# A tuned FFT and two-layer-pair kernel: conversion blocks in other slots, a conversion's buffers in alternating roles, a copy of the first quad and some GpSimd tasks at other places

## The chip, the cores and the metric

The kernel runs on one core of one Trainium2 chip. The metric is the device time of one execution in microseconds (us). The engines are PE (TensorE), DVE (VectorE), ACT (ScalarE), POOL (GpSimd) and SP (SyncE, which here only issues DMAs).

## What is computed

The reference, cut to what matters:

```python
X = np.fft.fft(np.fft.fft(x, axis=1), axis=2).real        # x: 4 x 3072 x 256
xk = mu_k * X + (1 - mu_k) * X_prev                       # X_prev: X one token earlier
xr = mu_r * X + (1 - mu_r) * X_prev
k = np.maximum(xk @ w_k, 0)                               # 256 -> 1024
y = sigmoid(xr @ w_r) * (k * k @ w_v)                     # 1024 -> 256
h = y @ w_in                                              # 256 -> 2048
out = (h - np.tanh(h)) @ w_out                            # 2048 -> 256
```

The weight matrices w_k, w_r, w_v, w_in and w_out reach the chip as 64-bit floats and are turned into 32-bit floats there.

## The kernel before, in words

**Stages.** A first stage does the transform (up to about 98 us). Phase 1 (98 to 678 us) does the layer with w_k, w_v and w_r, phase 2 (678 us to the end) the layer with w_in and w_out. Both phases work on 12 pairs of token blocks (2 x 512 tokens). A pair is done in quads, 4 in phase 1 and 8 in phase 2; a quad is a 2 x 2 block product with seven sub-products instead of eight, whose left operands are called a11, a12, a22, s1, s2, s3, s4, and then the four products of the second matrix ("11", "12", "21", "22"), which for a quad are issued during the next one. Every sub-product is three matmuls (`mm3`, L318 to L320): each operand is split into a rounded part, "hi", made by an ACT cast, and the rest, "lo", a subtraction on DVE or POOL.

**A quad's chain.** PSUM banks X, Z and W hold the sums. In the order of the program: a11 goes into X, ACT copies it (s1 copy, L504); a12 goes into Z, s2 into X, and ACT copies X again (s2 copy, L523); DVE adds the first copy to Z (L519); ACT applies the nonlinearity to Z (L482), DVE multiplies (L531), ACT rounds (hi, L487) and DVE subtracts (lo, L489). s3 goes into X, ACT copies it a third time (s3 copy, L539), and DVE adds it to W (L549), which gives the next block. a22 then goes into X and s4 into W. A bank is written anew only when its last reader is done. In the very first quad there is no previous quad's product to fill the gaps.

**Slots.** All work that is not the chain (operands of the next pair, weight conversions, loads) is put into slots: `at(slot, ...)` files a task, `fill()` runs the tasks of the next slot, four times per quad: after the s2 copy, after the lo of block 11, after the nonlinearity of block 22, and after the hi of block 22. So a phase 1 pair n has the slots n.0 to n.15, written here as pair.slot. Within a slot the conversions stand ahead of the tasks of the next pair. Each engine executes its own instructions strictly in the order in which they were written.

**Conversions.** `convert` with `fine=True` takes a block through seven steps: a load of four 128 KB pieces into the tile raw (SP, L364); the absolute value of the high words into tile a (ACT, L372); four DVE steps on a and raw (L374, L376, L378, L380; the last writes tile b); the scaled low words into b, the last reader of raw (DVE, L382); then in the next slot a + b (POOL, L392), and in the slot after that the write of a to DRAM (SP, L411; called keep). w_in has eight such blocks, w_out eight, and one block of w_v is done in pair 0. For w_in and that w_v block `x_room` gives one buffer of raw and one each of a and b (cva, cvb). The lists `early` and `free` (slots 0, 2, 6, 9 to 15 of each pair) say where the steps go.

**Pair 11** also prepares phase 2: `weights2` loads a w_in block into the tile wf (one buffer, SP L801) and a w_out block into another, and splits them (ACT L351, POOL L352 and L428 to L431, for the first two w_out blocks DVE L352); `left2` loads the stored pair (L791) and splits it (ACT L582, POOL L584; sums L592 to L595 on POOL).

**Pair 0's tasks.** `both_tasks` prepares the operands of pair n + 1: differences d0 to d3 (POOL L684), mixes k0 to k3 (DVE L689), scaled differences m0 to m3 (ACT L694), +0 to +3 (POOL L695), +s1 to +s4 (POOL L592 to L595), and the splits a11 to s4 (ACT L582, POOL L584) and x0 to x3 (ACT L351, POOL L352).

Of the kernel before, what the change touches and what calls it, by code (L numbers as in the profile page):

```python
# [7 lines left out]
F32 = mybir.dt.float32  # L8
# [314 lines left out]
def block(n, t):  # L323

    g, i = divmod(n, 6)
    m, j = divmod(i, 3)
    return (2 * g + t, 3 * m + 2) if j == 2 else (2 * g + j, 3 * m + t)


class Kernel:  # L330
    def __init__(self, tc, **dram):
        self.tc, self.nc = tc, tc.nc
        self.V, self.A, self.G, self.T = self.nc.vector, self.nc.scalar, self.nc.gpsimd, self.nc.tensor
        self.__dict__.update(dram)
        self.slots, self.now = {}, 0
        self.pend, self.odd = None, 0

    def at(self, slot, *stages):

        for k, f in enumerate(stages):  # L340
            if f:
                self.slots.setdefault(slot + k, []).append(f)
# [55 lines left out]
    def x_room(self):  # L398
        raw = self.xp.tile([128, 512, 2], I32, tag="raw", name="raw", bufs=1)
        def more():  # L400
            a, b = (self.xp.tile([128, 512], F32, tag=f"cv{x}", name=f"cv{x}", bufs=1) for x in "ab")
            return [a, b, b]
        return raw, more

# [62 lines left out]
    def quad(self, ph, n, q, nq, S, W, w2, done, extra=None):  # L467

        V, A, T = self.V, self.A, self.T
        ALU, ACT = mybir.AluOpType, mybir.ActivationFunctionType
        M = {}
        def P(ps, k, start, stop=True):
            i = RIGHT[k]
            mm3(T, ps, [W[:, 0, i], W[:, 1, i]], [S[k][:, 0], S[k][:, 1]], start, stop)
        bank = lambda tag, name: self.ps.tile([128, TOK], F32, tag=tag, name=name, bufs=1)
        ctile = lambda: self.act.tile([128, TOK], F32, tag="c", name="c", bufs=4)
        stile = lambda: self.act.tile([128, TOK], F32, tag="s", name="s", bufs=3)
        def bend(src):  # L480
            t = ctile()
            A.activation(t, src, ACT.Tanh if ph == 2 else ACT.Relu)  # L482
            return t
        gate = V.tensor_sub if ph == 2 else V.tensor_mul
        def hi(blk, g):
            M[blk] = self.act.tile([128, 2, TOK], F32R, tag="m", name=f"m{blk}", bufs=4)
            A.copy(M[blk][:, 0], g)  # L487
        def lo(blk, g):
            V.tensor_sub(M[blk][:, 1], g, M[blk][:, 0].bitcast(F32))  # L489
        p, self.pend = self.pend, None  # L490
        def late(*names):
            for k in names:
                if p:
                    p["late"][k]()
        self.odd ^= 1
        X, Z = bank(f"x{self.odd}", "x"), bank("z", "z")
        r = None
        P(X, "a11", True)
        if ph == 1:
            late("t21", "g21")  # L500
        else:
            late("t21", "c12", "g21")
        s1 = stile()
        A.copy(s1, X)  # L504
        if ph == 1:
            late("c12", "h21")
        else:
            late("t12", "h21", "g12")
        self.second(p, "11")
        P(Z, "a12", True)  # L510
        Wb = None
        if p is None:
            Wb = bank("w", "w")
            P(Wb, "s1", True)
        late("l21")
        if ph == 2:
            late("h12")
        P(X, "s2", False)
        V.tensor_add(Z, Z, s1)  # L519
        if ph == 2:  # L520
            late("l12")
        s2 = stile()
        A.copy(s2, X)  # L523
        if ph == 1:
            self.fill()
            late("t12", "g12")
        t11 = bend(Z)
        if ph == 2:
            self.fill()
        self.second(p, "22")  # L530
        gate(Z, Z, t11)  # L531
        if ph == 1:
            late("h12", "l12")
        P(X, "s3", False)
        hi("11", Z)
        if extra:
            r = extra(bank(f"x{1 - self.odd}", "r"))
        s3 = stile()
        A.copy(s3, X)  # L539
        lo("11", Z)  # L540
        self.fill()
        if r:
            r()
        if ph == 1:
            self.second(p, "21")
        if Wb is None:
            Wb = bank("w", "w")
            P(Wb, "s1", True)
        V.tensor_add(Z, Wb, s3)  # L549
        t22 = bend(Z)  # L550
        self.fill()
        self.second(p, "12")
        gate(Z, Z, t22)  # L553
        hi("22", Z)
        if ph == 1:
            self.fill()
            lo("22", Z)
        else:
            self.second(p, "21")
            lo("22", Z)  # L560
            self.fill()
        P(X, "a22", False)
        P(Wb, "s4", False)
        st = {}
        def t21():
            st["t21"] = bend(X)
        def c12():
            st["c12"] = Wb if ph == 1 else ctile()
            V.tensor_add(st["c12"], Wb, s2)
        def t12():  # L570
            st["t12"] = bend(st["c12"])
        self.pend = dict(n=n, q=q, nq=nq, m=M, w=w2, done=done, late=dict(
            t21=t21, c12=c12, t12=t12,
            g21=lambda: gate(X, X, st["t21"]), h21=lambda: hi("21", X), l21=lambda: lo("21", X),  # L574
            g12=lambda: gate(st["c12"], st["c12"], st["t12"]), h12=lambda: hi("12", st["c12"]), l12=lambda: lo("12", st["c12"])))  # L575
# [123 lines left out]
    def phase1(self):  # L699
        V, A, T = self.V, self.A, self.T  # L700
# [16 lines left out]
        def wv_task(q):  # L717
# [2 lines left out]
                t.append(self.kp.tile([128, TOK], F32, tag="xk", name="wv", bufs=4))  # L720
                self.nc.sync.dma_start(out=t[0], in_=self.wf[q])
            return [f, lambda: self.split(self.WV[q], t[0], self.G)]
        for r in (self.r0, self.r1):
            self.at(0, r[2])
        for q in range(3):
            self.at((0, 2, 6)[q], *wv_task(q))
        at = self.at
        for q, where in ((3, (0, 3, 5, 6, 8, 9, 10, 11)),):
            steps, out = self.convert(self.chunk_rows(self.wv, (q, q + 4)), [lambda a, q=q: self.split(self.WV[q], a, self.G)], self.x_room, V, True)
            for w, f in zip(where, steps + [lambda out=out: [f() for f in out]]):  # L730
                at(w, f)
        free = iter([16 * n + k for n in range(6, NP) for k in (0, 2, 6, 9, 10, 11, 12, 13, 14, 15)])
        for q in range(8):
            steps, out = self.convert(self.chunk_rows(self.w_out, (q, q + 8)), self.keep(12 + q), self.y_room, self.G, True)
            when = [next(free) for _ in steps[1:]]
# [4 lines left out]
        early = [16 * n + k for n in range(1, 6) for k in (0, 2, 6, 9, 10, 11, 12, 13, 14, 15)][2:]  # L740
        for q in range(8):
            steps, out = self.convert(self.quad_rows(self.w_in, q, HID2 // 2), self.keep(4 + q), self.x_room, self.G, True)
            when = early[8 * q:8 * q + 6] if q < 6 else [next(free) for _ in steps[1:]]
            at(early[8 * q - 3] + 1 if 0 < q < 6 else when[0] - 4, steps[0])
            for w, f in zip(when, steps[1:]):
                at(w, f)
            at(when[-1] + 1, *out)
        for n in range(NP):
            z = 16 * n
            if n == 0:  # L750
                for t, (f0, f1, f2) in ((3, self.r_task(0, 1, 0)), (4, self.r_task(0, 1, 1))):
                    at(t, f0, f1, f2)
            if n % 6 == 2:
                at(z + 4, lambda n=n: self.swap_rows(block(n, 1)[0]))
            if n + 1 < NP:
                u = self.both_tasks(n + 1)
                early = {0: "d0", 2: "d1", 4: "k0 d3", 5: "k1 m0", 6: "a11 d2 +0", 7: "k3 a12", 8: "k2 m1 a22", 9: "+s1 +1 m3"}
                if n == 0:
                    early = {0: "d0", 2: "d1", 4: "k0", 5: "k1 m0", 6: "a11 d3 +0", 7: "d2 a12", 8: "k3 m1", 9: "k2 a22 +1 m3 +s1"}
                for k, names in {**early, 10: "m2 s1 +s3 +3", 11: "+s2 +2", 12: "s3 +s4", 13: "s2", 14: "s4", 15: "x0", 16: "x1", 18: "x2", 19: "x3"}.items():  # L760
                    for name in names.split():
                        at(z + k, u[name])
                if n % 6 == 1:
                    at(z + 12, lambda n=n: self.swap_rows(block(n + 1, 0)[0]))
            for q in range(4):
                if n + 1 == NP and q == 1:
                    self.open2()
                w2 = [[self.WV[q][:, s, 256 * c:256 * c + 256] for s in range(2)] for c in range(2)]
                k = 4 * n + q - 1
                self.quad(1, n, q, 4, self.S[n], self.TK[q], w2, done, (lambda ps: r_block(ps, k)) if k >= 0 else None)  # L770
# [164 lines left out]
```

## Time and profile before

| | |
|---|---|
| median of 3 runs | 1674.95 us (1673.28 to 1676.17) |
| the profiled execution, whole | 1671.78 us |
| its span, first to last instruction | 1670.0 us |
| PE busy | 1633.8 us, 98% |
| DVE busy | 1274.7 us, 76% |
| ACT busy | 1135.8 us, 68% |
| POOL busy | 579.7 us, 35% |
| mean granted clock of PE | 0.992 of full speed |

The profile shows one execution, so its rows add up to its own time and not to the median. A row of the timeline has the start, the length, the engine, the line, the operation with output and input, and in brackets the idle time of the engine ahead of it and what ended that.

### The profile page before, as it was taken

How to read it: one execution, taken by the hardware profiler on the slowest of the kernel's cores; microseconds unless marked ns; L12 is line 12 of the kernel's file. 1: busy time of each engine (PE TensorE's matmuls, PEld its weight loads, DVE VectorE, ACT ScalarE, POOL GpSimd, SP SyncE). 2: the span in 40 equal slices, each digit the busy share in tenths (PEclk: the TensorE clock that was granted, in tenths of full speed). 3: DMA queues.
4: the chain of work that ended last, by engine and by line, in shares of the span. 5: the costliest groups of instructions: out<-in, count | busy, mean ns of one | idle time of the engine just before them, and what ended most of it. 6: DMA issues, size and time to landing. Idle time of an engine off the chain costs nothing.

```text
span 1670.0 us, 21330 instructions
## 1 busy us (share of the span) xinstructions
PE 1633.8 (98%) x7466; PEld 1352.9 (81%) x7466; DVE 1274.7 (76%) x2005; ACT 1135.8 (68%) x2162; POOL 579.7 (35%) x489
## 2 busy tenths in 40 slices
PE   7989999999999997999999999999999999999998
PEld 7967888888887885788888888888888888888887
DVE  7987888888888885777777777777777777777776
ACT  4876777777777775786666666666666666666665
POOL 0237676666667664481202020212112121212100
PEclk8999999999999998999999999999999999999999
DMA  9611001111111113211010101010101010101000
GB/s 328 160 41 39 32 33 45 45 58 45 64 46 63 35 35 108 82 39 51 1 51 1 51 1 51 1 51 1 51 1 51 1 51 1 51 1 51 1 26 26
DMA packets 39452, 77.96 MB, mean 47 GB/s; under 512 B 4512, under 2 KB 11808, under 8 KB 39344
## 3 DMA queue, kind: packets, MB, share of 16 engines
q1 hardware_dynamic: 37760, 72.41, 13.0%
q0 software_dynamic: 864, 3.41, 1.1%
q8 instruction: 58, 0.95, 0.2%
q10 hardware_dynamic: 720, 0.79, 0.1%
q14 instruction: 50, 0.41, 0.1%
HBM read 46.39 MB, written 30.20 MB: 46 GB/s over the span
## 4 chain that ended last, share of the span: by engine, by line
PE 92%; DVE 2%; issue 1%; ACT 1%; POOL 1%; DMA 1%; SPq 1%; ACTq 0%; DVEq 0%; POOLq 0%
PE o L319 15%; PE o L318 15%; PE o L320 15%; PE x L318 8%; PE x L319 8%; PE x L320 8%; PE w L318 4%; PE w L319 4%; PE w L320 4%; PE z L318 2%; PE z L319 2%; PE z L320 2%; PE r L319 1%; PE r L320 1%; PE r L318 1%
## 5 line engine op out<-in xcount | busy, mean ns | idle before, releaser
L489 DVE TENSOR_TENSOR m<-z,m 128x512 fp32r<-128x512 f32 x288 | 198.5, 689 | 139.6 <-ACT m L487 139.6
L319 PE MATMUL o<-m,WO 128*128 128x512 f32 x768 | 298.9, 389 | 0.0
L320 PE MATMUL o<-m,WO 128*128 128x512 f32 x768 | 298.8, 389 | 0.0
L318 PE MATMUL o<-m,WO 128*128 128x512 f32 x768 | 298.8, 389 | 0.0
L584 POOL TENSOR_TENSOR a<-xk,a 128x512 fp32r<-128x512 f32 x69 | 91.1, 1321 | 594.5 <-ACT a L582 592.7
L482 ACT ACTIVATE c<-z 128x512 f32<-128x512 f32 x288 | 172.9, 600 | 146.2 <-DVE z L549 145.6
L487 ACT CAST m<-z 128x512 fp32r<-128x512 f32 x288 | 169.2, 588 | 143.3 <-DVE z L553 79.7
L584 POOL TENSOR_TENSOR s<-xk,s 128x512 fp32r<-128x512 f32 x92 | 122.7, 1336 | 174.0 <-ACT s L582 174.0
L319 PEld LDWEIGHTS o<-m,WO 128*128 128x128 f32 x768 | 144.1, 188 | 30.2 <-DVE m L489 0.3
L318 PEld LDWEIGHTS o<-m,WO 128*128 128x128 f32 x768 | 144.1, 188 | 30.0
L320 PEld LDWEIGHTS o<-m,WO 128*128 128x128 f32 x768 | 144.1, 188 | 29.9
L553 DVE TENSOR_TENSOR z<-z,c 128x512 f32<-128x512 f32 x144 | 100.5, 698 | 70.8 <-ACT c L482 70.7
L318 PE MATMUL o<-m,wv 128*128 128x512 f32 x384 | 150.8, 393 | 0.0
L319 PE MATMUL o<-m,wv 128*128 128x512 f32 x384 | 150.6, 392 | 0.0
L320 PE MATMUL o<-m,wv 128*128 128x512 f32 x384 | 150.3, 391 | 0.0
L523 ACT COPY s<-x 128x512 f32<-128x512 f32 x144 | 84.6, 588 | 58.2 <-PE x L320 57.4
L504 ACT COPY s<-x 128x512 f32<-128x512 f32 x144 | 84.9, 590 | 57.2 <-PE x L320 57.1
L549 DVE TENSOR_TENSOR z<-w,s 128x512 f32<-128x512 f32 x144 | 100.5, 698 | 27.6 <-PE w L320 12.1
L531 DVE TENSOR_TENSOR z<-z,c 128x512 f32<-128x512 f32 x144 | 100.2, 696 | 26.9 <-ACT c L482 26.3
L574 DVE TENSOR_TENSOR x<-x,c 128x512 f32<-128x512 f32 x144 | 99.5, 691 | 10.0 <-ACT c L482 9.9
L575 DVE TENSOR_TENSOR c<-c 128x512 f32<-128x512 f32 x96 | 67.2, 700 | 49.9 <-ACT c L482 49.9
L489 DVE TENSOR_TENSOR m<-x,m 128x512 fp32r<-128x512 f32 x144 | 98.7, 685 | 2.6
(205 smaller groups left out, 4057.6 us busy)
## 6 DMA issues: line engine op xcount, KB each, us to landing
spill<-r SPq DMA_DIRECT2D x48, 256.0 KB
xk<-spill SPq DMA_DIRECT2D x48, 256.0 KB
out<-o SPq DMA_DIRECT2D x22, 512.0 KB
xr<-x SPq DMA_DIRECT2D x8, 512.0 KB
raw<-w_in SPq DMA_DIRECT2D x32, 128.0 KB
cv<-w_out SPq DMA_DIRECT2D x16, 256.0 KB
wf<-wf SPq DMA_DIRECT2D x16, 256.0 KB
wf<-cva SPq DMA_DIRECT2D x11, 256.0 KB
```

The lines of the kernel that those rows point to most:

```text
L318: T.matmul(ps, w[0], m[0], start=start, stop=False, skip_group_check=True)
L319: T.matmul(ps, w[0], m[1], start=False, stop=False, skip_group_check=True)
L320: T.matmul(ps, w[1], m[0], start=False, stop=stop, skip_group_check=True)
L482: A.activation(t, src, ACT.Tanh if ph == 2 else ACT.Relu)
L487: A.copy(M[blk][:, 0], g)
L489: V.tensor_sub(M[blk][:, 1], g, M[blk][:, 0].bitcast(F32))
L504: A.copy(s1, X)
L531: gate(Z, Z, t11)
L549: V.tensor_add(Z, Wb, s3)
L553: gate(Z, Z, t22)
L574: g21=lambda: gate(X, X, st["t21"]), h21=lambda: hi("21", X), l21=lambda: lo("21", X),
L584: eng.tensor_sub(S[name][:, 1], src(), S[name][:, 0].bitcast(F32))
```

## The change

Four edits:

1. The eight w_in blocks are spread otherwise: before, six of them lay in pairs 1 to 5 and two in pairs 10 and 11; now seven lie in pairs 1 to 5 and one in pairs 10 and 11, at the place where the seventh stood. In pairs 1 to 5 a block now follows its predecessor one step of the list sooner.
2. The two buffers cva and cvb change roles from one conversion to the next, so that a block's absolute value goes into the tile that was its predecessor's b.
3. In the first quad of the kernel the s3 product and its copy stand directly behind the s2 copy.
4. In pair 0 d0, d1, +1, +2, +3, s1 and two xr splits stand in later slots.

```diff
     def x_room(self):
         def more():
-            a, b = (self.xp.tile([128, 512], F32, tag=f"cv{x}", name=f"cv{x}", bufs=1) for x in "ab")
+            a, b = (self.xp.tile([128, 512], F32, tag=f"cv{x}", name=f"cv{x}", bufs=1) for x in ("ab", "ba")[self.turn])
+            self.turn ^= 1
             return [a, b, b]
...
         A.copy(s2, X)
+        s3 = None
+        if p is None:
+            P(X, "s3", False)
+            s3 = stile()
+            A.copy(s3, X)
...
-        P(X, "s3", False)
+        if s3 is None:
+            P(X, "s3", False)
...
-        s3 = stile()
-        A.copy(s3, X)
+        if s3 is None:
+            s3 = stile()
+            A.copy(s3, X)
...
-        for r in (self.r0, self.r1):
-            self.at(0, r[2])
+        self.at(2, self.r0[2], self.r1[2])
...
-            when = early[8 * q:8 * q + 6] if q < 6 else [next(free) for _ in steps[1:]]
-            at(early[8 * q - 3] + 1 if 0 < q < 6 else when[0] - 4, steps[0])
+            when = early[7 * q - q // 6:7 * q - q // 6 + 6] if q < 7 else [next(free) for _ in steps[1:]]
+            at(early[7 * q - 2] + 1 if 0 < q < 7 else when[0] - 4, steps[0])
...
+                rest = {9: "+s1 +1 m3", 10: "m2 s1 +s3 +3", 11: "+s2 +2", 12: "s3 +s4", 13: "s2", 14: "s4", 15: "x0", 16: "x1", 18: "x2", 19: "x3"}
                 if n == 0:
-                    early = {0: "d0", 2: "d1", 4: "k0", 5: "k1 m0", 6: "a11 d3 +0", 7: "d2 a12", 8: "k3 m1", 9: "k2 a22 +1 m3 +s1"}
+                    early = {2: "d0", 3: "d1", 4: "k0", 5: "k1 m0", 6: "a11 d3 +0", 7: "d2 a12", 8: "k3 m1"}
+                    rest = {**rest, 9: "k2 a22 m3 +s1", 10: "+1 m2 +s3", 11: "s1 +s2", 12: "s3 +s4 +3", 13: "s2 +2"}
```

With the new list the first steps of the w_in blocks (the absolute value on ACT) and the sums on POOL stand as follows; in both versions the sum is one slot behind the last DVE step, and a block's load waits for the last DVE step of the block ahead, since raw has one buffer.

| block | before: first step, sum | after: first step, sum |
|---|---|---|
| 0 | 1.6, 1.14 | 1.6, 1.14 |
| 1 | 2.0, 2.12 | 1.15, 2.11 |
| 2 | 2.14, 3.10 | 2.12, 3.3 |
| 3 | 3.12, 4.3 | 3.9, 3.15 |
| 4 | 4.10, 5.0 | 4.0, 4.12 |
| 5 | 5.6, 5.14 | 4.13, 5.7 |
| 6 | 10.14, 11.10 | 5.9, 5.15 |
| 7 | 11.10, 12.0 | 10.14, 11.10 |

The rows below give the order of instructions on an engine. Line numbers of the changed kernel are one to ten higher (L373 is the old L372, L393 the old L392, L593 the old L584, L603 the old L594, L811 the old L801).

First place: SP in pair 11, before the change. raw is the tile of block 7, wf the weights for phase 2, `wf<-cva` the keep of block 6.

```order
L801 DMA wf<-wf 128x512
L791 DMA xk<-spill 128x512 x4
L364 DMA raw<-w_in 128x256 x4
L801 DMA wf<-wf 128x512 x2
L411 DMA wf<-cva 128x512
```

The same place after the change: the four loads of raw are gone, so the two weight loads stand directly behind the stored pair.

```order
L811 DMA wf<-wf 128x512
L801 DMA xk<-spill 128x512 x4
L811 DMA wf<-wf 128x512 x2
L413 DMA wf<-cva 128x512
```

Second place: ACT in pair 2, slots 11 and 12, after the change. L373 is the absolute value of block 2; the row behind it is the cast of s3 for the next pair, then come the two nonlinearities (w, z) of the quad.

```order
L525 COPY s<-x 128x512
L373 ACTIVATE cvb<-raw 128x512
L591 CAST s_2439<-xk 128x512
L484 ACTIVATE c<-w 128x512
L484 ACTIVATE c<-z 128x512
```

POOL at the same place after the change: L393 is the sum of block 1, which reads cvb, L603 the sum +s2.

```order
L602 TENSOR_TENSOR xk<-xk 128x512
L704 TENSOR_TENSOR xt<-xt,y_0_112 128x512
L393 TENSOR_TENSOR cva<-cva,cvb 128x512
L603 TENSOR_TENSOR xk<-xk 128x512
```

Before the change L392 of block 1 stood two rows further down, in slot 12, and the absolute value of block 2 (L372) in slot 14; now the sum is filed in slot 11 and the absolute value in slot 12.

Third place: ACT in the first quad, before the change. The xr casts are the split of the first xr operand, `c<-z` is the nonlinearity of block 11, L539 the s3 copy.

```order
L504 COPY s<-x 128x512
L523 COPY s<-x 128x512
L351 CAST xr<-xt 128x512 x2
L482 ACTIVATE c<-z 128x512
L487 CAST m_1231<-z 128x512
L539 COPY s<-x 128x512
```

After the change the s3 copy (L530) stands ahead of the nonlinearity, and the casts stand two and three slots later.

```order
L506 COPY s<-x 128x512
L525 COPY s<-x 128x512
L530 COPY s<-x 128x512
L484 ACTIVATE c<-z 128x512
L489 CAST m_1226<-z 128x512
```

On PE nothing moves: the s3 product already followed the s2 product there in the first quad.

## Rows read from the trace of the kernel before

**Rows 1.** The page, busy time by engine: us, share, instructions.

```profile
PE 1633.8 (98%) x7466; PEld 1352.9 (81%) x7466; DVE 1274.7 (76%) x2005; ACT 1135.8 (68%) x2162; POOL 579.7 (35%) x489
```

**Rows 2.** Waits of PE, whole span: us in total, times, longest.

```profile
PE z L318 <- DVE m L489: 9.8, 4, 6.9
```

**Rows 3.** Timeline of PE in pair 11 and the start of phase 2.

```profile
640.65 0.39 PE L318 MATMUL x<-a,TK 128*128 128x512 f32 x1
...
651.99 0.39 PE L320 MATMUL w<-s,TK 128*128 128x512 f32 x1
655.75 0.80 PE L318 MATMUL x<-a,TK 128*128 128x512 f32 x1 [3.38 <-ACT r L715]
...
666.52 0.80 PE L318 MATMUL z<-a,TK 128*128 128x512 f32 x1 [6.88 <-DVE m L489]
...
677.53 0.39 PE L318 MATMUL x<-a,TI 128*128 128x512 f32 x1
```

**Rows 4.** Timelines of ACT, DVE and POOL in pair 11.

```profile
654.17 0.51 ACT L351 CAST TI<-wf 128x384 fp32r<-128x384 f32 x1 [5.82 <-DMA wf<-wf]
...
662.12 0.66 ACT L372 ACTIVATE cva<-raw 128x512 f32<-128x512 f32 x1 [5.93 <-POOL xk L593]
...
663.37 1.09 DVE L352 TENSOR_TENSOR WO<-wf,WO 128x512 fp32r<-128x512 f32 x1 [12.93 <-ACT WO L351]
...
639.17 0.52 POOL L431 TENSOR_TENSOR t<-wf,t 128x128 f32<-128x128 f32 x1
...
648.43 1.39 POOL L352 TENSOR_TENSOR TI<-t,TI 128x512 fp32r<-128x512 f32 x1 [3.60 <-ACT TI L351]
...
678.45 4.24 POOL L584 TENSOR_TENSOR s<-xk,s 128x512 fp32r<-128x512 f32 x3
```

**Rows 5.** Timeline of SP's issues in pair 11.

```profile
648.70 1.76 SPq L364 DMA_DIRECT2D raw<-w_in  x4
650.55 0.85 SPq L801 DMA_DIRECT2D wf<-wf  x2
660.04 0.32 SPq L411 DMA_DIRECT2D wf<-cva  x1
```

**Rows 6.** Timelines of ACT, PE and POOL in pair 0.

```profile
102.47 0.60 ACT L482 ACTIVATE c<-z 128x512 f32<-128x512 f32 x1
...
104.96 0.50 PE L318 MATMUL x<-a,TK 128*128 128x512 f32 x1 [2.41 <-ACT s L539]
...
135.60 1.73 POOL L592 TENSOR_TENSOR xk<-xk 128x512 f32<-128x512 f32 x1
...
137.36 0.62 ACT L582 CAST s<-xk 128x512 fp32r<-128x512 f32 x1 [2.73 <-POOL xk L592]
...
139.24 0.50 PE L318 MATMUL z<-a,TK 128*128 128x512 f32 x1 [2.26 <-DVE m L489]
```

**Rows 7.** A stretch of pair 0: length, busy by engine, granted clock, DMA share.

```profile
140.00:144.00 4.00, 4.00 (x12) 3.12 (x12) 2.97 (x6) 2.80 (x6) 4.00 (x4) 0.57 0.01 4
```

**Rows 8.** Timelines of SP, POOL and ACT at the end of pair 1.

```profile
194.17 1.78 SPq L364 DMA_DIRECT2D raw<-w_in  x4
...
196.47 1.29 POOL L392 TENSOR_TENSOR cva<-cva,cvb 128x512 f32<-128x512 f32 x1
...
196.96 0.62 ACT L351 CAST xr<-xt 128x512 fp32r<-128x512 f32 x1
```

**Rows 9.** Timelines of ACT, POOL, DVE and PE in pair 2, slots 11 to 13.

```profile
236.23 0.62 ACT L582 CAST s<-xk 128x512 fp32r<-128x512 f32 x1
...
236.54 1.30 POOL L594 TENSOR_TENSOR xk<-xk 128x512 f32<-128x512 f32 x1
...
238.74 0.69 DVE L489 TENSOR_TENSOR m<-w,m 128x512 fp32r<-128x512 f32 x1
...
240.25 0.39 PE L318 MATMUL w<-s,TK 128*128 128x512 f32 x1
```

**Rows 10.** Line L378 from 160 to 690 us: duration in ns, least, median, most.

```profile
L378 DVE SCALAR_TENSOR_TENSOR cva<-raw,cva x8: 680/683/1719, 185.2 to 673.2; 128x512 int32<-128x512 int32 x8
```

More of the change, by code (lines that the diff above doesn't have):

```diff
@@ L335, in __init__ @@
         self.slots, self.now = {}, 0
+        self.turn = 0
         self.pend, self.odd = None, 0
@@ L756, in phase1 @@
                 u = self.both_tasks(n + 1)
-                early = {0: "d0", 2: "d1", 4: "k0 d3", 5: "k1 m0", 6: "a11 d2 +0", 7: "k3 a12", 8: "k2 m1 a22", 9: "+s1 +1 m3"}
+                early = {0: "d0", 2: "d1", 4: "k0 d3", 5: "k1 m0", 6: "a11 d2 +0", 7: "k3 a12", 8: "k2 m1 a22"}
+                rest = {9: "+s1 +1 m3", 10: "m2 s1 +s3 +3", 11: "+s2 +2", 12: "s3 +s4", 13: "s2", 14: "s4", 15: "x0", 16: "x1", 18: "x2", 19: "x3"}
                 if n == 0:
-                    early = {0: "d0", 2: "d1", 4: "k0", 5: "k1 m0", 6: "a11 d3 +0", 7: "d2 a12", 8: "k3 m1", 9: "k2 a22 +1 m3 +s1"}
-                for k, names in {**early, 10: "m2 s1 +s3 +3", 11: "+s2 +2", 12: "s3 +s4", 13: "s2", 14: "s4", 15: "x0", 16: "x1", 18: "x2", 19: "x3"}.items():
+                    early = {2: "d0", 3: "d1", 4: "k0", 5: "k1 m0", 6: "a11 d3 +0", 7: "d2 a12", 8: "k3 m1"}
+                    rest = {**rest, 9: "k2 a22 m3 +s1", 10: "+1 m2 +s3", 11: "s1 +s2", 12: "s3 +s4 +3", 13: "s2 +2"}
+                for k, names in {**early, **rest}.items():
                     for name in names.split():
```

## The prediction

> **What bounds the kernel now.** I read the page first: PE is busy for 98% of the span [rows 1], so time can only come from where PE stands still or runs at a lower clock. The list of PE's waits is short, and its largest line is the product into Z that waits for DVE's lo: 9.8 us in 4 waits, one of them of 6.9 us [rows 2]. The timeline of PE shows where. In pair 11 an undisturbed quad runs from 640.65 to 652.21 (its last matmul starts at 651.99 and the next could follow 0.22 later), 11.56 us. The next quad starts only at 655.75, after 3.38 us of idle time, stands again for 6.88 us ahead of 666.52, and phase 2 starts at 677.53 [rows 3]. Undisturbed it would start at 652.21 + 11.56 = 663.77. So this place costs 13.76 us: 10.3 us of idle time and the rest in slow matmuls behind each of the two waits.
>
> The other engines tell why. ACT stood 5.82 us for the weight load wf, until 654.17, and then 5.93 us until 662.12 for the absolute value of block 7 [rows 4]. SP issued the wf load only at 650.55, right behind the four loads of raw at 648.70, which had to wait until block 6 was done with raw [rows 5]. The tile wf itself had been free since 639.17 + 0.52 = 639.69, when POOL's last reader of it ended [rows 4]. The second wait is put down to a POOL sum, but the tile is cva: its write to DRAM was issued at 660.04 [rows 5], and ACT could overwrite it 2.1 us later. Behind ACT's absolute value stood the cast of the w_out block, behind that DVE's subtraction, which idled for 12.93 us [rows 4], and behind that the gate of Z that PE's next product into Z needs.
>
> Pair 0 has smaller holes: 2.41 us ahead of a22 in the first quad and 2.26 us ahead of 139.24 [rows 6]. After the latter the clock was 0.57 of full speed for four microseconds, the lower of PE's two levels [rows 7]; that stretch did 4.00 x 0.57 = 2.3 us of work, so it cost 1.7 us more.
>
> **Pair 11.** The loads of raw and the block's ACT step, five DVE steps, POOL sum and write leave it. The wf load then follows the stored pair in SP's queue and waits for its tile alone, to 639.7. The old load took 654.17 - 650.55 = 3.6 us from issue to use, so the weights are there at 643.3, 5 us before POOL's split at 648.43 shows that ACT had got to that place. Both waits of ACT go. What is late next? In slot 10 DVE's subtraction for the w_out block stands ahead of the gate of Z; it took 1.09 us [rows 4], and the product into Z comes 9 matmuls after 652.21, near 654.25. The chain in front of it (nonlinearity, cast, subtraction, gate, hi, lo) ends within some tenths of that; I take 0.4 us. Sum: -13.4 us. The bounds: -14.8 if a further microsecond at the start of phase 2 goes too, -9 if POOL gets late there (below).
>
> **The first quad.** ACT now waits for the s3 product before the nonlinearity. That product ended at 104.96 - 2.41 = 102.55, since PE idled from there; the copy then blocks ACT for about 0.5 us, so the nonlinearity starts at 103.06 instead of 102.47 [rows 6]. The two xr casts that used to stand in its way are gone, but they weren't the last to finish. The a22 product may start 1.8 us sooner, but the s4 product behind it still waits for W's reader L549, which follows gate, hi and lo, and these follow the nonlinearity: +0.6 us. The second xr cast now lies in slot 3, ahead of the next quad's first nonlinearity on ACT, another 0.5 us on a DVE chain without gaps. I take +1.1 us, with bounds of 0 (both hidden) and +1.7 (a low clock for one stretch as in [rows 7]).
>
> **POOL's order in pair 0.** Before, ACT stood 2.73 us at 137.36 for +s1, which POOL ended at 135.60 + 1.73 [rows 6], because +1 came ahead of it; hi of block 22 was queued behind. Now +s1 comes one sum (1.73) sooner and its cast one slot later, behind that hi. The next thing late is the w_v cast in the same slot, which waits for DVE, and behind it the copy for the s2 product: PE will still stand there, between 0 and the old 2.26 us; I take 0.9. The low clock followed a wait of 2.26 us [rows 6, 7]; I take it that the shorter one doesn't bring it, so the 1.7 us go as well. Sum: 0.9 - 2.26 - 1.7 = -3.1 us; bounds 0 and -4.0.
>
> **Seven blocks in pairs 1 to 5.** The average load is no matter. What matters is that a block's first ACT step now lies closer to its predecessor's end, and that it overwrites the tile which the predecessor's POOL sum reads (before, the tile which the keep writes out).
>
> Block 1: its absolute value goes where ACT began a cast at 196.96; the sum of block 0 ended at 196.47 + 1.29 = 197.76 [rows 8]. The load began at 194.17; with the 3.6 us of the wf load it is there at 197.8. ACT stands 0.8 us, and the step itself takes 0.66 [rows 4]; the next copy that PE needs is up to 1.5 us late. Nothing was late before, so the price lies between 0 and 1.5; I take 0.6.
>
> Block 2: its absolute value displaces the cast at 236.23, and the sum of block 1 displaces the POOL row at 236.54, so it ends at 237.84 [rows 9]. ACT waits 1.6 us and works 0.6 more: all behind it is 2.2 us late. The lo of block 12, 238.74 + 0.69 = 239.43, moves to 241.6; it is the last reader of bank W, which PE overwrites from 240.25 on. So PE waits about 1.4 us, and DVE's conversion steps in slots 13 to 15 follow closely: 0.5 more. Bounds 0 and 3.6 (the same with a low clock of 1.7 us). The other hand-offs leave POOL two slots or more, or, for block 5, fall where ACT has idle time: 0, up to 1.5.
>
> Sum of this part: +2.5 us, bounds 0 and 6.6.
>
> **The sum.** -13.4 + 1.1 - 3.1 + 2.5 = -12.9 us against the profiled execution's 1671.8 us: 1658.9. That execution was 3.2 us shorter than the median of the three runs; from the median of 1674.95 the same step gives 1662 us.
>
> **A rule that speaks against the change.** Line L378 took 680 ns at best and 1719 ns at worst [rows 10]: up to 1.04 us of waiting while POOL was at work. The Trainium skill, "SBUF — State Buffer", section "Who interferes with whom", says why: DVE shares one port pair with GpSimd, an instruction of DVE with two SBUF inputs or in a two-port mode takes it, and the second to come blocks until the first is done. By that rule the row reads as a full block, and POOL is busiest in just the pairs that get the further block. Five steps that each meet a whole POOL operation of 1.4 us, an estimate by that page, would cost 7 us, against nothing where each meets a free port.
>
> **The rivals.**
> - *The port.* The seventh block's five DVE steps in pairs 1 to 5 each wait for POOL, and DVE has no slack. By the worst row that is 5 x 1.04 = 5.2 us more: 1667 us. For it: L378's spread. Against it: six blocks there left PE hardly a wait.
> - *POOL bounds the start of phase 2.* PE comes there at 663.8, but POOL's splits don't move with it: from 648.4 on it has some fourteen operations of 1.0 to 1.4 us (three of them took 4.24 together [rows 4]), and I get the lo of s2 at about 666.7, just when PE wants it. If each takes 0.3 us more, 4 us of the gain go: 1666 us.
> - *Pair 11 is not freed*, since wf waits for something other than SP's queue. The 5 us margin speaks against it. Then 1674.95 + 1.1 - 3.1 + 2.5 = 1675.5, no change.
> - *Slower: ACT's waits for POOL's sum.* If at four of the hand-offs ACT stands as long as for wf in pair 11, each costs 3.4 us of idle time and 1.7 of low clock, 20 us together: 1674.95 - 13.4 + 1.1 - 3.1 + 20.4 = 1680 us. It decides once POOL's sum comes more than about 3 us behind ACT at each; the rows show 0.8 and 1.6.
>
> **How the numbers follow.** The forecast, 1658 to 1665, gets 0.62; a larger gain 0.08; the port 0.10; POOL at phase 2 0.11; pair 11 not freed 0.05; slower 0.04. The prediction is 1662 us. Holding 8 in 10, the range goes from 1657.5 to 1668.5, which takes in the first two rivals. A measurement can tell some 0.2%, 3.3 us, from no change; so faster 0.91, same 0.05, slower 0.04.
>
> **What would show it.** In the new profile: no wait of PE above 1 us in pair 11, the wf load issued about 9 us ahead of its cast, and phase 2 starting some 13 us sooner; in the first quad a shorter wait ahead of a22 but s4 half a microsecond later; no 0.57 stretch near 140; new waits of ACT for POOL at the absolute values of blocks 1 and 2, with a PE wait ahead of W near 240. It is wrong if the wf cast waits again, if POOL's splits end late at the start of phase 2, or if pairs 1 to 5 lose more than 6 us.

## The result

The changed kernel took 1658.95 us (median of four executions) against 1674.84 us of the kernel before on the same chip. One of the four, the profiled one, was disturbed (3115 us, mean granted clock 0.852); the other three took 1657.64 to 1660.1 us, median 1657.81, and they alone give the ratio, 0.9903, 95% interval [0.9883, 0.9922]. In a second comparison it took 1658.63 against 1673.27, 0.9914 [0.99, 0.9927]. It is 0.9 to 1.0% faster, and the time lies inside the predicted range, 3 to 4 us below the predicted 1662.

All rows of the changed kernel below are from the profile of the second comparison (1659.56 us, span 1657.8).

The page's row of busy times, which answers to [rows 1]:

```profile
PE 1629.4 (98%) x7466; PEld 1349.0 (81%) x7466; DVE 1274.5 (77%) x2005; ACT 1134.8 (68%) x2162; POOL 578.7 (35%) x489
```

No engine has fewer instructions. What changed is how long PE stands, and how long it runs at the lower clock behind that (its busy time is 4.4 us less). The waits of PE from 100 to 700 us in the changed kernel (us in total, times, longest):

```profile
PE w L318 <- DVE z L558: 2.7, 2, 2.4
PE w L318 <- DVE m L491: 2.4, 2, 1.3
PE x L318 <- ACT s L506: 1.2, 3, 0.6
PE x L318 <- ACT s L525: 0.7, 1, 0.7
PE x L318 <- ACT s L530: 0.7, 1, 0.7
PE z L318 <- DVE m L491: 0.6, 2, 0.3
```

The wait for Z that was the largest line, 9.8 us with one of 6.9 [rows 2], is down to 0.6. The timeline of the changed kernel in pair 11 and at the start of phase 2, rows of SP, ACT, PE and POOL:

```profile
633.43 8.24 SPq L811 DMA_DIRECT2D wf<-wf  x2
...
640.81 0.52 POOL L433 TENSOR_TENSOR t<-wf,t 128x128 f32<-128x128 f32 x1
...
649.90 0.52 ACT L352 CAST TI<-wf 128x384 fp32r<-128x384 f32 x1
...
642.32 0.39 PE L318 MATMUL x<-a,TK 128*128 128x512 f32 x1
...
656.34 0.50 PE L318 MATMUL z<-a,TK 128*128 128x512 f32 x1 [0.26 <-DVE m L491]
...
665.99 0.39 PE L318 MATMUL x<-a,TI 128*128 128x512 f32 x1
...
669.45 0.40 PE L319 MATMUL x<-s,TI 128*128 128x512 f32 x1
...
666.56 3.79 POOL L593 TENSOR_TENSOR s<-xk,s 128x512 fp32r<-128x512 f32 x3
```

The two wf loads now stand right behind the stored pair: the group of two ends at 633.43 + 8.24 = 641.67, so SP was held only until POOL's last reader of the old wf had ended (640.81 + 0.52 = 641.33), and some 8 us later ACT casts from it at 649.90 without a bracket, that is, without idle time. From 642.32 to 665.99 PE takes 23.67 us, where it took 677.53 - 640.65 = 36.88 [rows 3]: 13.2 us less.

To split the span I took the start of the product into Z of a quad, less that of the first quad, in both traces:

| product into Z of | before | after | after less before, first quad as 0 |
|---|---|---|---|
| the first quad | 98.68 | 100.50 | 0 |
| the second quad | 110.44 | 113.69 | +1.43 |
| pair 2, first quad | 198.88 | 198.85 | -1.85 |
| pair 3, first quad | 245.69 | 247.36 | -0.15 |
| pair 11, third quad | 642.69 | 644.36 | -0.15 |
| phase 2, first quad | 679.70 | 668.34 | -13.18 |

The first quad itself starts 1.82 us later in this trace; that is the transform stage, which the change doesn't touch, and over twelve profiled executions of kernels that share it that start lay between 98.54 and 101.31.

### The profile page after: what moved, and what is told of

It is laid out like the page before. It is cut to its first block, busy times and chain, and to the rows that moved or that the text cites. A ratio compares the mean times of both kernels' runs of the same rounds, so it can differ in the third digit from the quotient of the medians.

```text
span 3113.3 us, 21330 instructions
## 1 busy us (share of the span) xinstructions
PE 3099.6 (100%) x7466; PEld 1958.3 (63%) x7466; DVE 1286.3 (41%) x2005; ACT 1162.2 (37%) x2162; POOL 560.8 (18%) x489
## 4 chain that ended last, share of the span: by engine, by line
PE 99%; DMA 1%; DVE 0%; SPq 0%; ACT 0%; issue 0%; DVEq 0%
PE o L320 16%; PE o L318 16%; PE o L319 16%; PE x L320 8%; PE x L318 8%; PE x L319 8%; PE w L319 4%; PE w L318 4%; PE w L320 4%; PE z L320 2%; PE z L318 2%; PE z L319 2%; PE s L195 1%; PE r L320 1%; PE r L318 1%; PE r L319 1%
## 5 line engine op out<-in xcount | busy, mean ns | idle before, releaser
L320 PE MATMUL o<-m,WO 128*128 128x512 f32 x768 | 471.1, 613 | 0.0
L318 PE MATMUL o<-m,WO 128*128 128x512 f32 x768 | 470.8, 613 | 0.0
L319 PE MATMUL o<-m,WO 128*128 128x512 f32 x768 | 470.2, 612 | 0.0
L593 POOL TENSOR_TENSOR a<-xk,a 128x512 fp32r<-128x512 f32 x69 | 88.6, 1285 | 1290.2 <-ACT a L591 1290.1
L318 PEld LDWEIGHTS o<-m,WO 128*128 128x128 f32 x768 | 191.1, 249 | 128.6 <-issue 92.6
L320 PEld LDWEIGHTS o<-m,WO 128*128 128x128 f32 x768 | 190.2, 248 | 128.7 <-issue 93.3
L319 PEld LDWEIGHTS o<-m,WO 128*128 128x128 f32 x768 | 190.6, 248 | 127.9 <-issue 90.8
L320 PE MATMUL o<-m,wv 128*128 128x512 f32 x384 | 259.1, 675 | 0.0
L318 PE MATMUL o<-m,wv 128*128 128x512 f32 x384 | 259.0, 674 | 0.0
L319 PE MATMUL o<-m,wv 128*128 128x512 f32 x384 | 258.9, 674 | 0.0
L593 POOL TENSOR_TENSOR s<-xk,s 128x512 fp32r<-128x512 f32 x92 | 117.7, 1279 | 553.1 <-ACT s L591 501.6
L484 ACT ACTIVATE c<-x 128x512 f32<-128x512 f32 x144 | 86.1, 598 | 338.8 <-PE x L320 338.8
L578 DVE TENSOR_TENSOR c<-w,s 128x512 f32<-128x512 f32 x96 | 66.4, 692 | 352.1 <-PE w L320 352.1
L521 DVE TENSOR_TENSOR z<-z,s 128x512 f32<-128x512 f32 x144 | 100.8, 700 | 235.5 <-PE z L320 235.5
L319 PEld LDWEIGHTS o<-m,wv 128*128 128x128 f32 x384 | 114.5, 298 | 65.0 <-issue 60.4
L318 PEld LDWEIGHTS o<-m,wv 128*128 128x128 f32 x384 | 114.5, 298 | 64.8 <-issue 60.2
```

The costliest lines, as they stand in the source:

```text
L318: T.matmul(ps, w[0], m[0], start=start, stop=False, skip_group_check=True)
L319: T.matmul(ps, w[0], m[1], start=False, stop=False, skip_group_check=True)
L320: T.matmul(ps, w[1], m[0], start=False, stop=stop, skip_group_check=True)
L593: eng.tensor_sub(S[name][:, 1], src(), S[name][:, 0].bitcast(F32))
```

## The experiments

Each was compared with the kernel before on the same chip. The brackets behind ratios are 95% intervals; "at phase 2" means the shift of the product into Z as in the table above.

**The changed kernel again**, unchanged, as the measure for the others.

> The changed kernel once more, with a profile. Theory A (the prediction's terms): pair 11 gives 13.4 us, the first quad costs 1.1, POOL's order in pair 0 gives 3.1, the hand-offs in pairs 1 to 5 cost 2.5; PE shows waits near 198 and 240 us. Theory B: the hand-offs cost nothing, since the engines that stand there have slack, and the first quad gains; PE shows no wait between 150 and 640 us. Both expect 1656 to 1662 us and no wait of PE above 1 us in pair 11.

Measured: 1658.63 against 1673.27, -14.6 us, 0.9914 [0.99, 0.9927]: theory A. PE waits 0.34 us near 200 and 1.06 us near 241, and the first quad loses time.

**Edits 1 and 2 alone**: the block list and the alternating buffers, without edits 3 and 4.

```diff
-            when = early[8 * q:8 * q + 6] if q < 6 else ...
+            when = early[7 * q - q // 6:7 * q - q // 6 + 6] if q < 7 else ...
...
+            self.turn ^= 1
```

> The kernel before with edits 1 and 2 alone (seven blocks in pairs 1 to 5, roles of the buffers alternating). Theory A: -13.4 + 2.5 = -10.9 us. Theory B: -13.4 to -14.8 us.

Measured: 1660.71 against 1673.27, -12.6 us, 0.9924 [0.991, 0.9938]. Nearly the whole gain is here. The interval, -10.4 to -15.1 us, takes in both theories; the trace decides for A. From pair 2 to pair 3 this kernel loses 2.89 us, with much the same two waits of ACT as the changed kernel (0.74 and 1.35 us), and at phase 2 it stands at -10.25.

**Edit 3 alone**: the s3 product and copy behind the s2 copy.

```diff
         A.copy(s2, X)
+        s3 = None
+        if p is None:
+            P(X, "s3", False)
+            s3 = stile()
+            A.copy(s3, X)
```

> The kernel before with edit 3 alone; the two xr casts stay in slot 0, now behind the s3 copy. Theory A: the nonlinearity of the first quad starts at 104.1 instead of 102.5, +1.6 us. Theory B: the a22 product no longer waits for the s3 copy, so up to 2.4 us are won, and nothing is lost.

Measured: 1674.49 against 1673.27, +1.2 us, 1.0006 [0.9998, 1.0015]. The time by itself can't be told from no change, but a gain of 2.4 us is out; its trace has the second quad 1.55 us later. Theory A.

**Edit 4 alone**: the xr splits in slots 2 and 3, the sums of pair 0 in their new slots.

```diff
-        for r in (self.r0, self.r1):
-            self.at(0, r[2])
+        self.at(2, self.r0[2], self.r1[2])
...
+                    rest = {**rest, 9: "k2 a22 m3 +s1", 10: "+1 m2 +s3", 11: "s1 +s2", 12: "s3 +s4 +3", 13: "s2 +2"}
```

> The kernel before with edit 4 alone. Theory A: the first nonlinearity starts 1.0 us sooner without the casts, the second cast costs 0.5 in slot 3, and the wait near 139 with its low clock shrinks by 3.1 us: -3.6 us. Theory B: the wait near 139 goes altogether, 2.3 + 1.7 = -4 us or more.

Measured: 1669.99 against 1673.27, -3.3 us, 0.998 [0.9971, 0.9989]. The interval, -1.8 to -4.9 us, holds both theories; in the trace the first product into Z of pair 2 stands at -3.66, and near 138 PE still stands 0.57 us, which is theory A. The parts add up: -12.6 + 1.2 - 3.3 = -14.7, where the whole gave -14.6.

**Edit 2 alone**: alternating buffers with the old block list.

> The kernel before with edit 2 alone. Theory A (ACT's wait of 5.9 us in pair 11 is for the write of cva to DRAM): the absolute value of block 7 starts at the end of POOL's sum, 660.0 instead of 662.1, and the wait of PE ahead of Z shrinks by 2.1: -2.1 us. Theory B (ACT waits for POOL's sums, as the releaser in the profile names one): no difference.

Measured: 1670.17 against 1674.01, -3.8 us, 0.9978 [0.9969, 0.9988]. The sign is theory A's; the size is larger than its 2.1, which lies just at the edge of the interval. In its trace ACT's wait ahead of the absolute value of block 7 is 3.85 us, put down to POOL's sum, instead of 5.93 [rows 4], and PE's wait for Z 4.4 instead of 6.9. The timeline of ACT and POOL in that kernel:

```profile
663.66 0.67 ACT L373 ACTIVATE cva<-raw 128x512 f32<-128x512 f32 x1 [3.85 <-POOL cvb L393]
...
662.36 1.28 POOL L393 TENSOR_TENSOR cvb<-cvb,cva 128x512 f32<-128x512 f32 x1
```

ACT starts where the sum ends (663.64). So the old wait was for the keep, and once that is out, POOL's sum is the next thing late. From the third quad of pair 11 to the second of phase 2 this trace takes 48.56 us, against 50.64 and 50.65 in the runs of edits 3 and 4 alone, whose pair 11 is the old one: 2.1 us less, theory A's number. Why the median gained more stays open; the profiled execution was the slowest of nine (1673.87), for a reason told in the last section.

**Edit 1 alone**: the new block list with fixed buffers.

> The kernel before with edit 1 alone: closer hand-offs, but cva always overwritten. Theory A: at blocks 1, 2 and 5 the absolute value waits for the keep's write, 2.1 us beyond POOL's sum; PE stands about 2 us more at two or three places, with a low clock at some: 5 to 9 us less gain than edits 1 and 2 together, so -4 to -8 us. Theory B: edit 2 counts in pair 11 alone, where the block is gone: -12.6 us as with both.

Measured: 1669.24 against 1674.01, -4.8 us, 0.9969 [0.9958, 0.998]: theory A. The timeline of ACT in that kernel at blocks 1 and 2, and the waits of PE from 150 to 420 us:

```profile
201.38 0.66 ACT L372 ACTIVATE cva<-raw 128x512 f32<-128x512 f32 x1 [2.84 <-DMA wf<-cva]
...
243.44 0.66 ACT L372 ACTIVATE cva<-raw 128x512 f32<-128x512 f32 x1 [3.42 <-DMA wf<-cva]
```

```profile
PE w L318 <- DVE m L489: 3.1, 1, 3.1
PE x L318 <- ACT s L504: 2.4, 1, 2.4
PE z L318 <- DVE m L489: 0.9, 1, 0.9
PE x L318 <- ACT r L715: 0.5, 1, 0.5
```

With one tile for every absolute value ACT waits for the keep to read it, at block 5 too (2.83 us). By the products into Z (as in the table above) this kernel stands +10.4 us by pair 11 and gets 13.0 back there: -2.6. With the swap the same stretch costs +2.8 (edits 1 and 2) instead of +10.4. So edit 2 is worth 7.6 us beside edit 1 by the traces (7.8 by the medians), and 2 to 4 without it: it is what makes the hand-offs cheap.

**The kernel before, with the load of block 7 three slots later**, behind the wf loads in SP's queue. This takes one of pair 11's two waits away by order alone.

```diff
-            at(early[8 * q - 3] + 1 if 0 < q < 6 else when[0] - 4, steps[0])
+            at(early[8 * q - 3] + 1 if 0 < q < 6 else when[0] - (1 if q == 7 else 4), steps[0])
```

> The kernel before with one load moved: the load of raw for block 7 is filed three slots later, behind the two weight loads in SP's queue; block 7 stays in pair 11. Theory A (the weight load waited behind raw in the queue): ACT's first wait and PE's 3.4 us go, the second wait stays, since POOL's sum and the write come as late after ACT as before, about 7 us: -5 to -6 us. Theory B (the eighth block's own work on ACT, DVE and POOL is what pair 11 lacks time for): 0 to -1 us.

Measured: 1668.51 against 1674.01, -5.5 us, 0.9967 [0.9954, 0.9979], in the middle of theory A's band (its trace gives less, -3.97 at phase 2). The timeline of SP and ACT in that kernel:

```profile
634.27 8.24 SPq L801 DMA_DIRECT2D wf<-wf  x2
651.19 2.33 SPq L364 DMA_DIRECT2D raw<-w_in  x4
657.59 0.33 SPq L411 DMA_DIRECT2D wf<-cva  x1
...
659.66 0.67 ACT L372 ACTIVATE cva<-raw 128x512 f32<-128x512 f32 x1 [6.09 <-DMA wf<-cva]
```

The wf wait and PE's wait of 3.38 us [rows 3] are gone; the keep is issued at 657.59 and ACT overwrites its tile at 659.66, 2.07 us later, which is the other wait, and here the trace names the keep itself.

**The changed kernel, absolute values of blocks 1 and 2 one step of the list later** (slots 2.0 and 2.13).

```diff
-            for w, f in zip(when, steps[1:]):
+            for w, f in zip([when[q in (1, 2)]] + when[1:], steps[1:]):
```

> The changed kernel with the absolute values of blocks 1 and 2 filed one step of the list later (2.0 and 2.13 instead of 1.15 and 2.12), all else the same. Theory A: ACT's waits for POOL's sum at these two places (0.8 and 1.3 us) go, and with them PE's waits of 0.3 and 1.1: 1.0 to 1.5 us faster than the changed kernel, -16 us against the kernel before. Theory B: DVE's steps behind them are late instead, no difference from the changed kernel.

Measured: 1656.36 against 1674.01, -17.7 us, 0.9895 [0.9882, 0.9909]. Its median lies 2.3 us below that of the changed kernel, but in another comparison, and the intervals overlap. The products into Z tell more: from pair 2 to pair 3 the changed kernel lost 1.70 us, this one gains 0.08 (-2.04 to -2.12). So theory A holds, with 1.8 us in place of its 1.0 to 1.5; at phase 2 it is -15.35 against -13.18, of which the rest lies in places where the two kernels are the same. The trace lists no wait of PE from 150 to 420 us there. Its ACT rows of the two steps, now without idle time:

```profile
198.80 0.66 ACT L373 ACTIVATE cva<-raw 128x512 f32<-128x512 f32 x1
...
237.41 0.68 ACT L373 ACTIVATE cvb<-raw 128x512 f32<-128x512 f32 x1
```

So what the hand-offs cost is ACT's standing at these two, and no more. (At block 5 ACT stands 0.61 us in the changed kernel and 0.62 here, and PE doesn't wait for it.)

**The changed kernel without edit 3.**

> The changed kernel without edit 3: the s3 copy of the first quad stands behind the hi of block 11 again, the other three edits stay. Theory A (edit 3 by itself costs, as its run alone gave 1.2 us): 1.1 to 1.6 us faster than the changed kernel, some 16 us faster than before. Rival B (together with edit 4 it pays, since edit 4 takes the xr casts out of the way and the a22 product comes 1.8 us sooner): 0 to 1.4 us slower than the changed kernel, 13.5 to 14.6 faster than before. The trace: by A the product into Z of the second quad stands at +0 us against the first, compared with the kernel before, by B at +1.4 or more.

Measured: 1656.31 against 1673.13, -16.8 us, 0.9901 [0.9886, 0.9916]. Theory A by the trace, and a little more: -1.31 at the second quad (against +1.43), -15.14 at phase 2, 1.96 ahead of the changed kernel; the times were taken in different comparisons, with intervals that overlap. The timeline of PE in the first quad of the changed kernel: its start, a22, s4, and the next quad's product into Z:

```profile
99.71 0.49 PE L318 MATMUL x<-a,TK 128*128 128x512 f32 x1
...
105.03 0.50 PE L318 MATMUL x<-a,TK 128*128 128x512 f32 x1 [0.68 <-ACT s L530]
...
108.41 0.80 PE L318 MATMUL w<-s,TK 128*128 128x512 f32 x1 [2.42 <-DVE z L558]
...
113.69 0.58 PE L318 MATMUL z<-a,TK 128*128 128x512 f32 x1
```

The same products without edit 3:

```profile
98.34 0.49 PE L318 MATMUL x<-a,TK 128*128 128x512 f32 x1
...
104.36 0.50 PE L318 MATMUL x<-a,TK 128*128 128x512 f32 x1 [1.37 <-ACT s L541]
...
105.40 0.80 PE L318 MATMUL w<-s,TK 128*128 128x512 f32 x1
...
109.58 0.39 PE L318 MATMUL z<-a,TK 128*128 128x512 f32 x1
```

Edit 3 brings a22 from 6.02 to 5.32 us after the quad's start and sends s4 from 7.06 to 8.70: the wait moves from a22 to s4 and grows, since s4 hangs on the nonlinearity, which now stands behind the s3 copy.

**Without edit 3 and with the later absolute values.** The two diffs above together.

> The changed kernel without edit 3 and with the absolute values of blocks 1 and 2 one step later. Theory A (the two gains lie at different places and add up): 17 to 19 us faster than before, from -3.6 in pair 0, -0.3 in the hand-offs, -13.5 in pair 11. Rival B (the gain in the first quad is lost again at the wait in slot 11 of pair 0): no faster than the kernel with the later absolute values alone, which gained 17.7 us in its own comparison.

Measured: 1654.71 against 1673.13, -18.4 us, 0.989 [0.9873, 0.9906]. The interval holds rival B's 17.7 as well, but the trace is theory A's: -3.69 at pair 2, no loss in the hand-offs (-0.05 to pair 3), and -16.88 at phase 2, against -15.35 with edit 3.

**The same, with the two xr casts in slots 1 and 2.**

```diff
-        self.at(2, self.r0[2], self.r1[2])
+        self.at(1, self.r0[2], self.r1[2])
```

> As the kernel without edit 3 and with the later absolute values, but the two xr casts of the first quad in slots 1 and 2 in place of 2 and 3. Theory A (in slot 3 the second cast stands ahead of the second quad's first copy, where PE stood 1.45 us in the run of edit 4 alone): 1 to 1.5 us faster than with slots 2 and 3. Rival B (the cast in slot 1 delays the nonlinearity of block 22 by 0.5 us, which all that follows waits for): no faster, up to 0.5 us slower.

Measured: 1653.87 against 1673.13, -19.3 us, 0.9886 [0.9871, 0.9901]. It has the lowest time of this study. Against slots 2 and 3 it is 0.8 us better by the median and 0.7 by the products into Z (-17.59 against -16.88), which two intervals that overlap can't tell from nothing. The trace shows what part is the edit's: the second quad's product into W, which waits for the DVE step behind ACT, comes 0.52 us sooner (20.30 against 20.82 us behind the first quad's product into Z). So theory A is right in kind, at half its size. It took its size from the wait for the s1 copy, 1.45 us in the run of edit 4 alone but 0.31 with slots 2 and 3 here. That copy started as late in both (10.8 us behind the first product into Z); PE came 1.1 us later here, since its granted clock from 104 to 108 us was 0.58 against 1.00.

## Why the prediction was right, and where its sizes were off

| term | predicted | trace |
|---|---|---|
| first quad | +1.1 | +1.43 |
| POOL's order in pair 0 | -3.1 | -1.85 - 1.43 = -3.28 |
| hand-offs, pairs 1 to 10 | +2.5 | -0.15 + 1.85 = +1.70 |
| pair 11 to phase 2 | -13.4 | -13.18 + 0.15 = -13.03 |
| sum | -12.9 | -13.18 |

The sum came out, and so did the main steps behind it. The term that was mis-sized is pair 11, because its price was read from one trace: against two other executions it is -14.55 (below).

**Pair 11.** Both steps of the chain hold. That wf waited in SP's queue behind raw, and not for its tile, is shown by the run with the later load; that the second wait was for the keep of block 6, although the trace put it down to a POOL sum, by the same run, whose trace names the keep, and by edit 2 alone, where the wait shrinks to the sum's. The chain of w_out cast, subtraction and gate left 0.26 us ahead of 656.34; I had taken 0.4.

**The median against the sum.** The sum fits the trace, but the median fell by 14.6 us in the second comparison and by 17.0 in the first (to 1657.81), not by 12.9. The second interval (12.2 to 16.7 us) holds the 12.9, the first (13.1 to 19.6) just misses it, so by the times the gap is hardly shown. The traces show where most of it lies: in a price of pair 11 that the one execution of before understated. After the wait of 6.88 us its next row to phase 2, 677.53 - 666.52, took 11.01 us [rows 3]. In the run of edit 3 alone, where nothing there is changed, it took 681.25 - 668.90 = 12.35, in that of edit 4 alone 12.31. The difference is the clock. The timeline of PE in the run of edit 3:

```profile
668.90 0.79 PE L318 MATMUL z<-a,TK 128*128 128x512 f32 x1 [7.08 <-DVE m L489]
...
681.25 0.39 PE L318 MATMUL x<-a,TI 128*128 128x512 f32 x1
```

Windows of that stretch (length, busy time of PE, PEld, DVE, ACT and POOL, then the granted clock), first of the run of edit 3, then of the kernel before:

```profile
668.00:672.00 4.00, 3.10 (x7) 2.48 (x8) 3.52 (x6) 1.76 (x5) 0.00 (x0) 0.50 0.00 0
672.00:676.00 4.00, 4.00 (x13) 3.15 (x12) 2.91 (x5) 3.33 (x7) 0.00 (x0) 0.66 0.01 2
```

```profile
668.00:672.00 4.00, 4.00 (x16) 3.23 (x15) 2.65 (x5) 2.17 (x5) 0.00 (x0) 0.83 0.01 2
672.00:676.00 4.00, 4.00 (x20) 3.30 (x19) 2.82 (x5) 3.22 (x7) 2.33 (x3) 1.00 0.00 0
```

Behind much the same wait PE ran at the lower of its two levels until about 674.7 in one execution (0.66 over four microseconds is 2.7 at half and 1.3 at full clock), 5.8 us, and until about 669.4, 2.8 us, in the other. By the same reading it was 5.7 us in the run of edit 4 alone, 5.4 in that of edit 2 and 3.2 in that of the later load, whose waits for Z were 6.55, 4.39 and 7.18. The term of -13.4 was sized from the shortest.

From the third quad of pair 11 to the second of phase 2 the trace of before takes 49.60 us, the runs of edits 3 and 4 alone 50.64 and 50.65, and the changed kernel 36.09 (36.09 to 36.15 in all seven traces with the new block list). So the term is -13.5 against the one and -14.55 against the other two, and with -14.55 the sum is +1.43 - 3.28 + 1.70 - 14.55 = -14.7, which is the fall of the second comparison. Five traces don't show how often each length comes, so how much of the gap this makes up on average is not shown.

**The first quad.** "+0.6 us" for s4 was right: 8.70 us after the quad's start against 106.00 - 97.88 = 8.12 before, +0.58. But it is a net of two parts that I did not see apart: edit 4, which clears the casts, brings s4 1.06 us forward (8.12 to 7.06), and edit 3 costs 1.64. "The two xr casts weren't the last to finish" missed the first.

The second term, 0.5 us for the second cast in slot 3, came too, but it doesn't show at the second quad's product into Z, since there the lower clock hides it: PE ran at that clock longer behind the 2.42 us wait than behind the 2.41 us before and lost 0.85 more up to 113.69. That the row shows about the predicted +1.1 is luck. The run with the later absolute values, whose first quad is the same, with the same 2.42 us wait, stands at only +0.59 there. The next place where PE waits for the chain in every trace is the second quad's product into W. The timeline of PE there, in the kernel before, the changed kernel, the one without edit 3 and with the later absolute values, and the one with the casts in slots 1 and 2:

```profile
120.03 0.50 PE L318 MATMUL w<-s,TK 128*128 128x512 f32 x1 [0.58 <-DVE z L549]
...
123.25 0.50 PE L318 MATMUL w<-s,TK 128*128 128x512 f32 x1 [0.32 <-DVE z L558]
...
119.71 0.50 PE L318 MATMUL w<-s,TK 128*128 128x512 f32 x1 [0.90 <-DVE z L551]
...
119.56 0.50 PE L318 MATMUL w<-s,TK 128*128 128x512 f32 x1 [0.84 <-DVE z L551]
```

| kernel | behind the first quad's product into Z | less before |
|---|---|---|
| before | 21.35 | 0 |
| edit 3 alone | 23.05 | +1.70 |
| edit 4 alone | 20.83 | -0.52 |
| the changed kernel | 22.75 | +1.40 |
| the changed kernel, later absolute values | 22.52 | +1.17 |
| without edit 3, later absolute values | 20.82 | -0.53 |
| the same, casts in slots 1 and 2 | 20.30 | -1.05 |

The last two rows give the second cast's price, 0.52 us. Edit 3 costs 1.70, with edit 4 or without it; the two together give +1.17, and the prediction's 0.6 + 0.5 = 1.1 is the same sum.

**POOL's order.** Right in each step. The timeline of the changed kernel, ACT and PE, and a window over the stretch of [rows 7]:

```profile
139.44 0.62 ACT L352 CAST wv<-cva 128x512 fp32r<-128x512 f32 x1 [0.51 <-DVE cva L393]
...
141.60 0.50 PE L318 MATMUL x<-s,TK 128*128 128x512 f32 x1 [0.58 <-ACT s L506]
```

```profile
140.00:144.00 4.00, 3.42 (x15) 2.47 (x14) 2.60 (x5) 3.48 (x8) 4.00 (x4) 1.00 0.02 4
```

The wait of 2.26 us is 0.58 (I took 0.9), for the cast and the copy that the prediction named, and the clock of 0.57 is 1.00: 0.58 - 2.26 - 1.7 = -3.4 against -3.28. Counted from the product into W of the table above to pair 2, it is -3.14 to -3.25 in all six traces that have edit 4.

**The hand-offs.** The timeline of the changed kernel at blocks 1 and 2, ACT, POOL and PE:

```profile
197.83 0.67 ACT L373 ACTIVATE cva<-raw 128x512 f32<-128x512 f32 x1 [0.80 <-POOL cvb L393]
...
237.80 0.66 ACT L373 ACTIVATE cvb<-raw 128x512 f32<-128x512 f32 x1 [1.34 <-POOL cva L393]
...
236.48 1.29 POOL L393 TENSOR_TENSOR cva<-cva,cvb 128x512 f32<-128x512 f32 x1
...
241.60 0.50 PE L318 MATMUL w<-s,TK 128*128 128x512 f32 x1 [1.06 <-DVE m L491]
```

ACT stood 0.80 and 1.34 us, predicted 0.8 and 1.6; PE stood 1.06 ahead of W, predicted 1.4. (At block 1 the load of raw, issued from 194.14 on, would be there at about the same time as POOL's sum, so that the releaser named there is not proof.) Block 1 cost 0.2 us by the products into Z, predicted 0.6, block 2 1.5, predicted 1.9. The same list cost 2.89 us from pair 2 to pair 3 in the run of edits 1 and 2: there DVE's first step of block 2 stood through two POOL operations, 2.23 us where the changed kernel has 0.98, and PE waited for DVE twice more (0.34 and 0.64 us). So 1.7 is the price of one execution, 2.9 of another, and the predicted 2.5 lies between.

```profile
243.08 2.23 DVE L375 TENSOR_SCALAR cvb<-cvb 128x512 f32<-128x512 f32 x1
```

**The rivals.** *The port*: false as a price of each block. The conversion steps on DVE from 150 to 426 us (grouped by line) summed to 23.7 us for six blocks before, 3.95 each, and to 27.0 for seven after, 3.86 each; no PE wait is left there once ACT's two are gone. But single steps did stand longer, 2.23 us in the run of edits 1 and 2 (above) and 3.91 in that of edit 2 (below). *POOL at phase 2*: false here, the matmul that had waited 0.53 us for POOL's s before starts at 669.45 with no idle time ahead; the split that it needs, the second of the three in POOL's row, runs from 667.80 for 1.30 us, to 669.10, so the margin was 0.35 us. *Pair 11 not freed* and *slower*: false, as above; ACT's three waits for POOL's sums were 0.80, 1.34 and 0.61 us. Edit 1 alone shows that the last was a real danger: with ACT waiting for the keep the stretch cost 10.4 us.

## What to carry to other kernels

For a wait in an in-order queue, ask also what stands ahead of the instruction, and not only what it waits for: moving one load three slots later won 5.5 us alone. When two uses of a buffer come closer together, swapping the roles of two tiles can change the wait from the end of a DMA that still reads the tile to the end of a neighbour's compute step, here 10.4 us down to 2.8. A price read from one trace carries that execution's clock; read the same stretch in several before a term is sized from it. And undo a change's parts one by one even after it has won: by the traces one of the four cost 1.5 to 2 us, and two steps filed one place later won 1.8 more.

## What the runs showed of the hardware that was not expected

A DVE step can stand through several POOL operations, not just one: two in the row of the run of edits 1 and 2 above, three in the run of edit 2 alone. The timeline of that run, far from the stretch that it changes:

```profile
427.26 3.91 DVE L375 TENSOR_SCALAR cv<-cv 128x512 f32<-128x512 f32 x1
...
427.10 1.32 POOL L586 TENSOR_TENSOR s<-xk,s 128x512 fp32r<-128x512 f32 x1
428.36 1.31 POOL L597 TENSOR_TENSOR xk<-xk 128x512 f32<-128x512 f32 x1
429.61 1.29 POOL L586 TENSOR_TENSOR s<-xk,s 128x512 fp32r<-128x512 f32 x1
...
431.84 0.50 PE L318 MATMUL w<-s,TK 128*128 128x512 f32 x1 [1.91 <-DVE z L551]
```

The step, 0.42 us at its shortest and 1.42 in the trace of before at this place, ended at 431.17, just behind the third POOL operation (429.61 + 1.29 = 430.90); PE stood 1.91 us for what was queued behind it and with the lower clock lost 3.0 us. In twelve traces of some 85 such steps each the next longest was 2.23. It fits the Trainium skill, "SBUF — State Buffer", "Who interferes with whom", by which the second to come blocks until the first is done, but there it is one instruction that holds the port; this row shows three in a row. That the port is the cause is inferred from the times and that section of the Trainium skill; no run here takes the POOL operations away.

The other surprise is that much the same waits are followed by the lower clock for unequal times: 2.8, 3.2, 5.7 and 5.8 us behind 6.6 to 7.2 us of idle time in pair 11, and in the first quad two executions with the same 2.42 us wait differ by 0.84 us at the next quad. A single trace shows one of these.
